# Token mixing two tiles behind the attention, with a batch's inner layer split behind the tile's normalisation

## The chip, the cores and the metric

The kernel runs on one core of one Trainium2 chip. The metric is the device time of one execution in microseconds (us); the time before is the median of three executions. Five engines matter: TensorE (PE, with its weight loads shown as PEld), VectorE (DVE), ScalarE (ACT), GpSimd (POOL), and SyncE (SP), which issues most of the DMAs. Each engine works through its own queue in the order in which the program was written; semaphores tie the queues together.

## The reference, cut to what matters

```python
# q, k, v: (8 batches, 8 heads, 576 positions, 64)
scores = q @ k.T / 8, masked to the 64 latest positions
attn   = softmax(scores) @ v                     # -> x: (8, 576, 512)
xt = x.transpose(0, 2, 1)
h  = np.maximum(xt @ w_tok1, 0.0) @ w_tok2       # token mixing, inner layer of 256
u  = x + h.transpose(0, 2, 1)
h2 = np.maximum(u @ w_ch1, 0.0) @ w_ch2          # channel mixing, inner layer of 1536
out = u + h2
```

So there is a windowed attention, then a token-mixing layer over the positions of each batch (two matrix products with a ReLU between), then a channel-mixing layer. The products of the two mixing layers are done with each operand split into a high part, rounded to a shorter mantissa, and the low remainder: three matmuls (high·high, low·high, high·low) stand for one.

## The kernel before, in words

**Tiles.** The 8 batches of 576 positions are cut into 36 attention tiles of 128 positions, nine to a pair of batches (`tile_blocks`, L65). Tiles 0 to 3 of a pair belong to its first batch, 5 to 8 to its second, and tile 4 holds 64 positions of each. So a batch's last attention tile is number 4 or 8 of its pair.

**Steps.** The loop of L462 makes step i (from -1 to 36). In step i stand the second half of the attention of tile i and the beginnings of later tiles:

- `pt_transpose(i, 0)`, `(i, 1)` (L297): four transposes each on PE into a PSUM tile `pp`, and a copy by ACT to `pt`. The index u in 0, 1 stands for the even and the odd heads.
- `softmax(i + 1, u)` and `softmax_exp(i + 1, u)` (L270, L288): DVE scales and masks the scores (`e`) and takes the row maximum (`nm`); ACT then runs four exponentials.
- `av(i, pts)` (L308): 32 small matmuls into `xp`. The first 16 read `pt(i, 0)`, the second 16 read `pt(i, 1)`. `norm(i)` (L325) then makes the tile's `x` on DVE.
- `qk(i + 2)` (L250): the scores `s` of the tile after next, 32 small matmuls.

Threaded through these are the token-mixing layer and the weight conversion:

- `split_x(n)` (L331): ACT casts `x` of tile n to `xhi`, POOL subtracts to give `xlo`. For a tile number 4 these are two casts and two subtractions on half the partitions each (L338, L339).
- `tok1(n)` (L423): tile n's part of the first token-mixing product, six matmuls of 512 columns into the two PSUM tiles `h` of its batch (four for a tile 4, whose second half belongs to the next batch and is added with tile 5, which then has ten). After a batch's last tile, `finish_h` (L364) makes the ReLU: two ACT instructions to `hhi`, two DVE instructions to `hlo`, and queues the batch's eight *pieces*.
- `tok2` (L380), one piece: two or three transposes of `x`, then six matmuls of 256 or 320 columns into one PSUM tile `up`, and a copy to `u` by ACT. There is a single `up` buffer until step 35, when `up_tags` gets four more (L471). `PIECES` (L44) says how many pieces a step runs in its first slot (behind the four exponentials of u = 0, L495) and its second (behind `qk`, L521); without an entry it is one and one.
- `JOBS` (L43) says in which steps weights are converted: one job in every step up to 5, then in the steps whose number three does not divide. In the step behind such a one ACT has a cast `w1hi` more.

**The plan.** `tok1_plan` (L456 to L460) gives tile n of the token mixing to step n + 1 from step 4 on, after a first stretch with one tile a step. `split_x(n)` stands at the end of step n, behind that step's `norm`, `qk` and second piece (L522 to L524), unless the plan lets it stand early, in the middle of a step (L489 to L492); it may only if tile n's `norm` was in an earlier step.

**After the loop** the last pieces are run, and then the channel mixing (L585 on): 9 chunks of 512 positions, each with 144 matmuls (`gp`, L593) and 144 more (`op`, L629), PE almost without a gap.

Of the kernel before, what the change touches and what calls it, by code (L numbers as in the profile page):

```python
# [40 lines left out]


JOBS = {i: 1 if i < 6 or i % 3 else 0 for i in range(-1, 37)}  # L43
PIECES = {32: (1, 0), 33: (1, 0), 34: (1, 0), 35: (3, 0), 36: (2, 1)}  # L44

TOK1_FROM, TOK1_SLOW, TOK2_FROM = 2, 4, 7

N_PE, N_EARLY = 7, 4

# [25 lines left out]
def mixer_kernel(ctx: ExitStack, tc: tile.TileContext, qh, kh, vh, wt1, wt2, wc1, wc2, out):  # L75
# [37 lines left out]
    with ExitStack() as actx:  # L113
# [8 lines left out]
        def load_k(i):  # L122
            p, t = divmod(i, TPP)
            if t in (0, 4):
                b = 2 * p + (t == 4)
                kbs[b] = pq.tile([P, H // 2, (NBLK + 1) * BLK], F32, name=f"k{b}", tag="k", bufs=2)
                if b != 0:
                    nc.sync.dma_start(kbs[b], kh[b])

        def load_q(i):  # L130
            qr = pq.tile([P, H // 2, 2, BLK], F32, name=f"q{i}", tag="q", bufs=5)
            nc.sync.dma_start(qr, qh[i])
            loaded[i] = [qr, None]

        def load_v(i):
            vt = pq.tile([P, 2, H, D], F32, name=f"v{i}", tag="v", bufs=3)
            nc.sync.dma_start(vt, vh[i])
            loaded[i][1] = vt
# [158 lines left out]
        def pt_transpose(i, u):  # L297
            pp = ps.tile([P, 4, P], F32, name=f"pp{i}_{u}", tag="pt")
            e = e_sb.pop((i, u))
            for h in range(4):  # L300
                nc.tensor.transpose(pp[:, h], e[:, h], ident)  # L301
            pt = pa.tile([P, 4, P], F32, name=f"pt{i}_{u}", tag="ptsb", bufs=4)
            nc.scalar.copy(pt, pp)  # L303
            return pt
# [13 lines left out]
        def recip(i):  # L318
            _, sm = st.pop(i)
            ri = pa.tile([P, H], F32, name=f"ri{i}", tag="ri", bufs=2)  # L320
            nc.vector.tensor_scalar_add(ri, sm, 1e-9)
            nc.vector.reciprocal(ri, ri)
            return ri

        def norm(i, xp, ri):  # L325
            x = pa.tile([P, H, D], F32, name=f"x{i}", tag="x", bufs=12)
            nc.vector.tensor_mul(x, xp, ri.unsqueeze(2).to_broadcast([P, H, D]))
            xs[i] = x.rearrange("p h d -> p (h d)")
# [17 lines left out]
        def tok1_part(i, b, rows, slot, first, last):  # L346
            xhi, xlo = xhl[i]
            if first:
                h_ps[b] = [ps.tile([P, C], F32, name=f"h{b}_{tt}", tag="h") for tt in range(NTT)]
            for tt in range(NTT):  # L350
                if rows is full:
                    combos = ((t1hi, xhi), (t1hi, xlo), (t1lo, xhi))
                else:
                    x = xhi if rows is top else xlo
                    combos = ((t1hi, x), (None, x))
                for n, (w, x) in enumerate(combos):
                    w, o = (t1z[:, rows is bottom], 0) if w is None else (w, slot * DT)
                    nc.tensor.matmul(h_ps[b][tt], w[:, o + tt * P:o + (tt + 1) * P], x,  # L358
                                     start=first and n == 0, stop=last and n == len(combos) - 1)
# [3 lines left out]
        def finish_h(b):  # L363
            hh = []  # L364
            for tt in range(NTT):
                hp = h_ps[b][tt]
                hi = pa.tile([P, C], F32R, name=f"hhi{b}_{tt}", tag=f"hhi{tt}", bufs=2)
                lo = pa.tile([P, C], F32R, name=f"hlo{b}_{tt}", tag=f"hlo{tt}", bufs=2)
                nc.scalar.activation(hi, hp, AF.Relu)
                nc.vector.scalar_tensor_tensor(out=lo, in0=hp, scalar=0.0, in1=hi.bitcast(F32),  # L370
                                               op0=ALU.max, op1=ALU.subtract)
                hh.append((hi, lo))
            h_ps.pop(b)
            for half in range(2):
                for ct in range(NCT):
                    pieces.append((b, half, ct, hh))
# [36 lines left out]
        def store_u():  # L413
            while stores:
                us, g0, n = stores.pop(0)
                a = 0
                while a < n:
                    j, o = divmod(g0 + a, CHUNK)
                    m = min(n - a, CHUNK - o)
                    (nc.sync if g0 < (B - 1) * S - 320 else nc.scalar).dma_start(u_dram[j][:, :, o:o + m], us[:, :, a:a + m])  # L420
                    a += m

        def tok1(i):  # L423
            p, t = divmod(i, TPP)
            b0, b1 = 2 * p, 2 * p + 1
            if t < 4:
                tok1_part(i, b0, full, t, t == 0, False)
            elif t == 4:
                tok1_part(i, b0, top, 4, False, True)
                finish_h(b0)  # L430
            else:
                if t == 5:
                    tok1_part(i - 1, b1, bottom, 4, True, False)
                tok1_part(i, b1, full, t - 5, False, t == 8)
                if t == 8:
                    finish_h(b1)

        def run_pieces(k):
            for _ in range(min(k, len(pieces))):
# [15 lines left out]
        load_v(1)  # L455
        tok1_plan, n = {}, 0  # L456
        for i in range(TOK1_FROM, NT + 1):
            m = min(n + (1 if i < TOK1_SLOW else 2), i)
            tok1_plan[i] = range(n, m)
            n = m  # L460
        qk(0)
        for i in range(-1, NT + 1):  # L462
            if 0 <= i and i + 2 < NT:
                load_v(i + 2)
            if 3 <= i + 3 < NT:
                load_q(i + 3)
            if i + 4 < NT:
                load_k(i + 4)
            store_u()
            n_jobs = JOBS[i]  # L470
            if i == NT - 1:  # L471
                up_tags += [("s", 2), ("pt", 2)]
            have = len(pieces)
            n_pieces = PIECES.get(i, (1, 1) if i >= TOK2_FROM else (0, 0))
            pts = []
            early = i < N_EARLY
            if 0 <= i < NT:
                pts.append(pt_transpose(i, 0))
                if early:
                    pts.append(pt_transpose(i, 1))  # L480
            if i + 1 < NT:
                softmax(i + 1, 0)
            if early and i > 0:
                norm(*normed.pop())
            if 0 <= i < NT:
                ri = recip(i)
            while to_finish:
                job_finish()
            for n in tok1_plan.get(i + 1, ()):  # L489
                last_use = n - NX + ((n - NX) % TPP == 4)  # L490
                if n < i and last_use not in tok1_plan.get(i, ()):
                    split_x(n)  # L492
            if i + 1 < NT:
                softmax_exp(i + 1, 0)
            run_pieces(min(have, n_pieces[0]))  # L495
            have = min(have, len(pieces))
            if not early:
                for _ in range(n_jobs):
                    job_convert_a()
            if 0 <= i < NT and not early:  # L500
                pts.append(pt_transpose(i, 1))
            if i + 1 < NT:
                softmax(i + 1, 1)
            if early:
                for _ in range(n_jobs):
                    job_convert_a()
            for n in tok1_plan.get(i, ()):
                tok1(n)
            if i + 1 < NT:
                softmax_exp(i + 1, 1)  # L510
            for _ in range(n_jobs):
                job_convert_b()
            if 0 <= i < NT:
                xp = av(i, pts)
                if i + 1 < N_EARLY:
                    normed = [(i, xp, ri)]
                else:
                    norm(i, xp, ri)
            if i + 2 < NT:
                qk(i + 2)  # L520
            run_pieces(min(have, n_pieces[1]))  # L521
            for n in tok1_plan.get(i + 1, ()):  # L522
                if n not in xhl:
                    split_x(n)  # L524
            while to_load and len(to_convert) < 2 and i < NT - 2:
                job_load()
            if i == NT - 1:
                while to_convert or to_convert_b or to_finish:
                    job_convert_a()
                    job_convert_b()  # L530
                    job_finish()
                qctx.close()
                pu = uctx.enter_context(tc.tile_pool(name="pu", bufs=1, side="right", reuse_waits="tile"))
                ul = {0: load_u(0, pu)}
# [136 lines left out]
```

## Time and profile before

| what | value |
|---|---|
| median of three runs | 878.97 us (878.91 to 879.26) |
| the profiled execution's own time | 880.53 us |
| its span, first to last instruction | 878.7 us |
| mean granted TensorE clock | 0.993 |
| busy over the span | PE 850.6, PEld 702.6, DVE 378.3, ACT 307.5, POOL 105.3 us |
| start of step 0's `av` / of step 35's `av` | 14.80 / 268.34 us |
| first `gp` matmul of the channel mixing | 283.36 us |

The profile is one execution. A row of the timeline gives start, duration, engine, line, operation, output<-inputs, the shape (partitions x elements), a count, and in brackets the engine's idle time ahead of it with what ended it. Consecutive instructions of one kind are merged into a row. PE's matmuls are pipelined: a matmul of 512 columns shows 0.39 us, but the next one starts 0.23 us behind it. So it is starts that tell PE's pace, and an idle time of PE is shown only as far as it goes beyond the end of the matmul before. A row of the waits gives who waited for whom, the total in us, the number of times and the longest. The steps below are named by their number i; the attention's steps take about 7 us each.

### The profile page before, as it was taken

Reading aid. Unit: us, or ns where it says so; the run is one execution under the profiler, and the core shown is the slowest. Engines: PE = TensorE matmul, PEld = TensorE weight load, DVE = VectorE, ACT = ScalarE, POOL = GpSimd, SP = SyncE. Lnnn points to the kernel's source line nnn. Section 1 sums busy time; section 2 is a strip of 40 time slices with the busy share of each in tenths; the row PEclk is TensorE's granted clock in tenths of the full one; section 3 lists DMA queues with packets and bytes.
Section 4 is the critical chain, followed back from the end, with each engine's and each line's share of the span. In section 5 each row is a group of like instructions: output and inputs, shape, how many; then the busy total and the mean of one; then the engine's idle time right before and its main releaser. Section 6 shows DMA issues by size and latency. Waiting matters only on the chain.

```text
span 878.7 us, 14566 instructions
## 1 busy us (share of the span) xinstructions
PE 850.6 (97%) x6002; PEld 702.6 (80%) x6002; DVE 378.3 (43%) x701; ACT 307.5 (35%) x966; POOL 105.3 (12%) x109
## 2 busy tenths in 40 slices
PE   6889999989989999999999999999999999999998
PEld 4668878868879878888888888888888888888887
DVE  5979878878874795220220220220220220220211
ACT  5778777878875341120120220220220220220200
POOL 3433343433332000000000000000000000000000
PEclk9989999999999999999999999999999999999999
DMA  9566667567535531100100100100100101100001
GB/s 322 195 203 229 200 235 244 183 235 246 182 127 167 182 106 57 60 7 30 60 13 24 60 13 25 60 13 25 60 12 31 54 13 39 46 13 37 0 13 37
DMA packets 39907, 84.69 MB, mean 96 GB/s; under 512 B 5281, under 2 KB 18337, under 8 KB 37921
## 3 DMA queue, kind: packets, MB, share of 16 engines
q1 hardware_dynamic: 37728, 81.93, 27.9%
q10 hardware_dynamic: 2112, 1.84, 0.6%
q8 instruction: 47, 0.77, 0.4%
q14 instruction: 20, 0.16, 0.1%
HBM read 64.09 MB, written 19.66 MB: 95 GB/s over the span
## 4 chain that ended last, share of the span: by engine, by line
PE 83%; DVE 8%; ACT 4%; POOL 2%; issue 2%; DMA 1%; POOLq 0%; SPq 0%; DVEq 0%; ACTq 0%
PE op L629 33%; PE gp L593 30%; PE h L358 5%; PE up L400 4%; PE s L266 4%; PE xp L313 3%; PE up L393 2%; POOL xlo L94 2%; PE pp L301 1%; ACT u L405 1%; DVE r L200 1%; DMA u_dram<-u 1%; DVE c L197 1%; ACT xhi L91 1%; ACT e L294 1%
## 5 line engine op out<-in xcount | busy, mean ns | idle before, releaser
L597 ACT ACTIVATE ghi<-gp 128x512 fp32r<-128x512 f32 x108 | 64.5, 597 | 432.2 <-PE gp L593 431.9
L629 PE MATMUL op<-ghi,w2lo 128*128 128x512 f32 (+1 forms) x444 | 170.9, 385 | 1.9 <-DVE w2lo L94 1.9
L629 PE MATMUL op<-glo,w2hi 128*128 128x512 f32 (+1 forms) x444 | 170.9, 385 | 0.0
L629 PE MATMUL op<-ghi,w2hi 128*128 128x512 f32 (+1 forms) x444 | 170.8, 385 | 0.0
L593 PE MATMUL gp<-ulo,w1hi 128*128 128x512 f32 x432 | 168.1, 389 | 0.0
L593 PE MATMUL gp<-uhi,w1hi 128*128 128x512 f32 x432 | 168.1, 389 | 0.0
L593 PE MATMUL gp<-uhi,w1lo 128*128 128x512 f32 x432 | 168.0, 389 | 0.0
L598 DVE SCALAR_TENSOR_TENSOR glo<-gp,ghi 128x512 fp32r<-128x512 f32 x108 | 74.5, 690 | 187.7 <-ACT ghi L597 187.7
L631 DVE TENSOR_TENSOR uf<-op,uf 128x512 f32<-128x512 f32 (+1 forms) x37 | 25.0, 677 | 243.7 <-PE op L629 243.7
L629 PEld LDWEIGHTS op<-ghi,w2lo 128*128 128x128 f32 x444 | 83.9, 189 | 18.8 <-DVE w2lo L94 2.3
L629 PEld LDWEIGHTS op<-ghi,w2hi 128*128 128x128 f32 x444 | 83.8, 189 | 16.6
L629 PEld LDWEIGHTS op<-glo,w2hi 128*128 128x128 f32 x444 | 83.8, 189 | 16.5
L593 PEld LDWEIGHTS gp<-uhi,w1hi 128*128 128x128 f32 x432 | 81.1, 188 | 16.9
L593 PEld LDWEIGHTS gp<-uhi,w1lo 128*128 128x128 f32 x432 | 81.1, 188 | 16.8
L593 PEld LDWEIGHTS gp<-ulo,w1hi 128*128 128x128 f32 x432 | 81.1, 188 | 16.8
L294 ACT ACTIVATE e<-e,nm 128x128 f32<-128x128 f32 x232 | 90.5, 396 | 8.0 <-DVE nm L286 8.0
L94 POOL TENSOR_TENSOR xlo<-x,xhi 128x512 fp32r<-128x512 f32 x32 | 42.9, 1340 | 66.3 <-ACT xhi L91 66.0
L313 PEld LDWEIGHTS xp<-v,pt 128*64 128x64 f32 x1152 | 37.4, 137 | 16.4 <-ACT pt L303 6.3
L266 PE MATMUL s<-k,q 64*64 64x128 f32 x1152 | 43.7, 287 | 2.4 <-DVE c L197 1.9
L313 PE MATMUL xp<-v,pt 128*64 128x64 f32 x1152 | 43.1, 226 | 2.7 <-ACT pt L303 2.4
L294 ACT ACTIVATION_READ_ACCUMULATOR e<-e,nm 128x1 f32 x232 | 44.8, 193 | 0.0
L303 ACT COPY pt<-pp 128x512 f32<-128x512 f32 x72 | 41.8, 587 | 6.4 <-PE pp L301 6.3
(79 smaller groups left out, 1002.7 us busy)
## 6 DMA issues: line engine op xcount, KB each, us to landing
v<-vh SPq DMA_DIRECT2D x36, 512.0 KB, 3.8
raw<-wc SPq DMA_DIRECT2D x32, 384.0 KB, 4.4
q<-qh SPq DMA_DIRECT2D x36, 256.0 KB, 4.6
k<-kh SPq DMA_DIRECT2D x7, 1280.0 KB, 8.0
out<-uf SPq DMA_DIRECT2D x35, 256.0 KB, 2.3
uf<-u_dram SPq DMA_DIRECT2D x8, 1024.0 KB, 5.6
u_dram<-u SPq DMA_DIRECT2D x7, 512.0 KB, 3.7
k<-kh SPq DMA_DIRECT2D x5, 256.0 KB, 6.2
```

The costliest lines, as they stand in the source:

```text
L94: eng_lo.tensor_sub(lo, src, hi.bitcast(F32))
L266: nc.tensor.matmul(s[u][half * BLK:(half + 1) * BLK, j], qt[r, j, half], kbs[b][r, j, n * BLK:n * BLK + P], start=not on_pe, stop=True, sk ...
L294: nc.scalar.activation(e[:, h], src[:, h], AF.Exp, bias=nm[:, g:g + 1], scale=by, accum_out=sm[:, g:g + 1])
L303: nc.scalar.copy(pt, pp)
L313: nc.tensor.matmul(xp[half * BLK:(half + 1) * BLK, h], pts[h % 2][:, h // 2, half * BLK:(half + 1) * BLK], vt[:, half, h], start=True, sto ...
L358: nc.tensor.matmul(h_ps[b][tt], w[:, o + tt * P:o + (tt + 1) * P], x, start=first and n == 0, stop=last and n == len(combos) - 1)
L400: nc.tensor.matmul(up[:, :n], hx[:, cs], w[:, tt * S + s0:tt * S + s0 + n], start=False, stop=(k == 6), skip_group_check=True)
L593: nc.tensor.matmul(gp, w[:, ct * F + ft * P:ct * F + (ft + 1) * P], x[:, ct], start=(k == 0), stop=(k == 3 * NCT - 1))
L597: nc.scalar.activation(ghi, gp, AF.Relu)
L598: nc.vector.scalar_tensor_tensor(out=glo, in0=gp, scalar=0.0, in1=ghi.bitcast(F32), op0=ALU.max, op1=ALU.subtract)
L629: nc.tensor.matmul(op, w[:, ct, ft], x[:, cols], start=(k == 0), stop=(k == 3 * NFT - 1))
L631: nc.vector.tensor_add(uf[:, ct, cols], op, uf[:, ct, cols])
```

## The change

It does four things.

1. `tok1_plan` gives tile n of the token mixing to step n + 2 in place of n + 1, up to step 33. In step 34 the lag is made up: this step has tiles 32 and 33. By this, `split_x(n)` moves from the end of step n to the middle of step n + 1 (L489 to L492 apply now).
2. `finish_h` is no longer called inside `tok1`; the batch is put on a list, and the two ACT and two DVE instructions are written behind the step's `norm`, ahead of `qk`.
3. `PIECES` has two pieces in the first slot of step 34 in place of one.
4. What follows from 1: a batch's eight pieces become available one step later. Steps 15 and 24 now have no piece to run in either slot (before: 23 and 32); step 32 and step 33 have one each (before: none and one), step 34 two (before: one).

```diff
-PIECES = {32: (1, 0), 33: (1, 0), 34: (1, 0), 35: (3, 0), 36: (2, 1)}
+PIECES = {32: (1, 0), 33: (1, 0), 34: (2, 0), 35: (3, 0), 36: (2, 1)}
...
-TOK1_FROM, TOK1_SLOW, TOK2_FROM = 2, 4, 7
+TOK1_FROM, TOK1_SLOW, TOK1_CATCH_UP, TOK2_FROM = 2, 4, 34, 7
...
+        to_finish_h = []
...
                 tok1_part(i, b0, top, 4, False, True)
-                finish_h(b0)
+                to_finish_h.append(b0)
...
                 if t == 8:
-                    finish_h(b1)
+                    to_finish_h.append(b1)
...
-            m = min(n + (1 if i < TOK1_SLOW else 2), i)
+            m = min(n + (1 if i < TOK1_SLOW else 2), i - (i < TOK1_CATCH_UP))
...
                     norm(i, xp, ri)
+            while to_finish_h:
+                finish_h(to_finish_h.pop(0))
             if i + 2 < NT:
                 qk(i + 2)
```

Three places in the order of the instructions show it. The first is ACT's queue from the second piece's copy of step 11 to the second `pt` of step 12, a step with a weight cast. Numbers behind a name are the tile's (and u), or the batch's and the half's and column block's for `u` and `up`; the last number is the buffer's. Before:

```order
L405 COPY u1_0_1435<-up1_0_1_1504 128x256
L91 CAST xhi11_1514<-x11_1484 128x512
L303 COPY pt12_0_1529<-pp12_0_1524 128x512
L91 CAST w1hi_66<-w10_1462 128x384
L294 ACTIVATE e13_0_1533,sum13_1532<-e13_0_1533,nm13_1531 128x128 x4
L405 COPY u1_0_1435<-up1_0_2_1545 128x256
L303 COPY pt12_1_1560<-pp12_1_1555 128x512
```

The same stretch of ACT's queue now:

```order
L406 COPY u1_0_1427<-up1_0_1_1498 128x256
L304 COPY pt12_0_1519<-pp12_0_1514 128x512
L92 CAST w1hi_66<-w10_1456 128x384
L92 CAST xhi11_1531<-x11_1478 128x512
L295 ACTIVATE e13_0_1523,sum13_1522<-e13_0_1523,nm13_1521 128x128 x4
L406 COPY u1_0_1427<-up1_0_2_1539 128x256
L304 COPY pt12_1_1554<-pp12_1_1549 128x512
```

The cast `xhi` of tile 11 went behind the first `pt` and the weight cast; between the first row and the last stand the same five instructions as before.

The second place is ACT's queue in step 34, from the odd heads' exponentials of tile 34 to the second `pt`. Before:

```order
L294 ACTIVATE e34_1_4006,sum34_3976<-e34_1_4006,nm34_3975 128x128 x4
L91 CAST xhi33_4062<-x33_4042 128x512
L303 COPY pt34_0_4071<-pp34_0_4066 128x512
L294 ACTIVATE e35_0_4075,sum35_4074<-e35_0_4075,nm35_4073 128x128 x4
L405 COPY u6_0_3997<-up6_0_1_4085 128x256
L303 COPY pt34_1_4104<-pp34_1_4099 128x512
```

The same stretch now:

```order
L295 ACTIVATE e34_1_3982,sum34_3948<-e34_1_3982,nm34_3947 128x128 x4
L370 ACTIVATE hhi6_0_4012<-h6_0_3534 128x512
L370 ACTIVATE hhi6_1_4016<-h6_1_3535 128x512
L92 CAST xhi33_4038<-x33_4010 128x512
L304 COPY pt34_0_4048<-pp34_0_4043 128x512
L295 ACTIVATE e35_0_4052,sum35_4051<-e35_0_4052,nm35_4050 128x128 x4
L406 COPY u6_0_4071<-up6_0_0_4062 128x256
L406 COPY u6_0_4071<-up6_0_1_4073 128x256
L304 COPY pt34_1_4092<-pp34_1_4087 128x512
```

Batch 6's two ReLU instructions now stand here (before, in step 32), and the copies of two pieces stand behind tile 35's exponentials in place of one.

The third place is PE's queue in step 34 around the pieces, up to the token mixing of batch 7. Before:

```order
L400 MATMUL up6_0_1_4085<-t2hi_134,hlo6_1_3910 128x256
L301 MATMUL pp34_1_4099<-ident_65,e34_1_4006 128x128 x4
L358 MATMUL h7_0_4009<-xhi33_4062,t1hi_132 128x512
L358 MATMUL h7_0_4009<-xlo33_4063,t1hi_132 128x512
L358 MATMUL h7_0_4009<-xhi33_4062,t1lo_133 128x512
L358 MATMUL h7_1_4010<-xhi33_4062,t1hi_132 128x512
L358 MATMUL h7_1_4010<-xlo33_4063,t1hi_132 128x512
L358 MATMUL h7_1_4010<-xhi33_4062,t1lo_133 128x512
L313 MATMUL xp34_4125<-v34_3862,pt34_0_4071 64x64 x8
```

The same place now, from the first piece's last matmul on:

```order
L401 MATMUL up6_0_0_4062<-t2hi_134,hlo6_1_4017 128x256
L394 MATMUL up6_0_1_4073<-ident_65,x27_3322 128x128
L394 MATMUL up6_0_1_4073<-ident_65,x28_3438 128x128
L401 MATMUL up6_0_1_4073<-t2hi_134,hhi6_0_4012 128x256
L401 MATMUL up6_0_1_4073<-t2lo_135,hhi6_0_4012 128x256
L401 MATMUL up6_0_1_4073<-t2hi_134,hlo6_0_4013 128x256
L401 MATMUL up6_0_1_4073<-t2hi_134,hhi6_1_4016 128x256
L401 MATMUL up6_0_1_4073<-t2lo_135,hhi6_1_4016 128x256
L401 MATMUL up6_0_1_4073<-t2hi_134,hlo6_1_4017 128x256
L302 MATMUL pp34_1_4087<-ident_65,e34_1_3982 128x128 x4
L359 MATMUL h7_0_4097<-xlo31_3849,t1hi_132 128x512
```

A second piece follows the first on PE directly, into the same single `up` buffer, and behind `pp34_1` stand sixteen `h` matmuls (tiles 32 and 33 with the half of 31) where six stood.

## The prediction

> **What bounds the kernel now.** I read the page first, for the share of each engine.
>
> ```profile
> PE 850.6 (97%) x6002; PEld 702.6 (80%) x6002; DVE 378.3 (43%) x701; ACT 307.5 (35%) x966; POOL 105.3 (12%) x109
> ```
>
> PE is the bound over the whole, but the change touches only the attention (to 283 us of 879), and there the question is what PE waits for. So I read the waits next.
>
> ```profile
> PEld h L358 <- POOL xlo L94: 9.6, 19, 1.2
> ...
> PEld h L358 <- POOL xhi L339: 5.8, 4, 2.0
> ...
> PE xp L313 <- ACT pt L303: 2.4, 5, 0.7
> ```
>
> PE's weight loads for the token mixing wait 9.6 + 5.8 = 15.4 us for `split_x`: this is the most that the change can remove. Five times `av` waits for `pt` from ACT. Whether the 15.4 us come back depends on how far behind that second wait is, so I read a steady step with a weight cast on the timeline, step 12: ACT's rows, then PE's.
>
> ```profile
> 97.18 0.37 ACT L405 COPY u<-up 128x256 f32<-128x256 f32 x1 [1.45 <-PE up L400]
> 97.45 0.62 ACT L91 CAST xhi<-x 128x512 fp32r<-128x512 f32 x1
> 97.97 0.59 ACT L303 COPY pt<-pp 128x512 f32<-128x512 f32 x1
> 98.44 0.52 ACT L91 CAST w1hi<-w 128x384 fp32r<-128x384 f32 x1
> 98.86 0.41 ACT L294 ACTIVATE e<-e,nm 128x128 f32<-128x128 f32 x1
> ...
> 100.41 0.36 ACT L405 COPY u<-up 128x256 f32<-128x256 f32 x1
> 100.66 0.59 ACT L303 COPY pt<-pp 128x512 f32<-128x512 f32 x1
> ```
>
> ```profile
> 98.96 0.47 PE L358 MATMUL h<-xhi,t1hi 128*128 128x512 f32 x1
> 99.50 0.50 PE L358 MATMUL h<-xlo,t1hi 128*128 128x512 f32 x1
> ...
> 100.85 1.15 PE L313 MATMUL xp<-v,pt 128*64 128x64 f32 x32
> ```
>
> PE loses about 0.3 us between the first `h` matmul and the one that reads `xlo`. Then `av` runs through without a break. But its second half, which reads the second `pt`, begins half a microsecond in, at about 101.35, and that `pt` ends at 101.25. ACT arrives 0.1 us ahead of PE. It got there without idling from 97.18 on, through 4.07 us of work that PE's piece of the step before released. A step without a weight cast has more room:
>
> ```profile
> 107.28 0.59 ACT L303 COPY pt<-pp 128x512 f32<-128x512 f32 x1
> ...
> 107.96 1.15 PE L313 MATMUL xp<-v,pt 128*64 128x64 f32 x32
> ```
>
> Here `pt` ends at 107.87 and the second half begins at about 108.45, 0.6 us later. So in the steady steps two waits stand almost in line, and the change removes only the first.
>
> **The steady steps (8 to 13, 17 to 22, 26 to 31).** The cast `xhi` moves on ACT from ahead of the first `pt` to behind it; the work between 97.18 and 101.25 stays the same. The first `pt` now follows the copy directly and has to wait for its transposes: four of them take 0.66 (the row at 258.19 below) from about the piece's end, the copy gives way after 0.27, so ACT idles at most 0.3 there; I take 0.15. In a step with a cast PE therefore gains the 0.1 that ACT is early and loses 0.15: 12 steps x 0.05 = +0.6. Five of the six without a cast have a wait for `xlo`, which goes: 5 x -0.3 = -1.5. In steps 10, 19 and 28 the ReLU now stands on ACT between the exponentials and the second piece's copy, and on DVE behind `norm` and ahead of the next tile's `e`; who waits for that copy is PE's next piece. ACT idles 1.45 us ahead of this copy (row 97.18), the two instructions take 1.07 (row 248.60 below), so it fits but for some 0.1 each: +0.3. On POOL `xlo` now stands behind the weight's subtraction, with most of a step until PE reads it, and on SP the stores of `u` are issued a step later, hundreds of us ahead of their loads: nothing for both. Sum -0.6, between -8 (nearly all waits of these steps return) and +2 (no gain, 12 bubbles).
>
> **Steps without pieces.** Before, these are 23 and 32, and the longest waits (2.0, 1.2) lie at them. Now they are 15 and 24, where PE has only transposes, `h`, `av` and `qk`, so ACT sets the pace, with the ReLU on top. I take -0.45 for each: -0.9, between -4 (two times 2.0) and +1. The start, steps 4 to 7, is bound by ACT and DVE in the same way, and there half the `h` work only moves later: +0.3, between -1.5 and +1.5.
>
> **The end, steps 32 to 35.** Up to step 31 PE has now done six `h` matmuls and two pieces fewer; they return here, and I follow the queues. Before, on PE:
>
> ```profile
> 256.07 1.15 PE L313 MATMUL xp<-v,pt 128*64 128x64 f32 x32
> 257.15 1.10 PE L266 MATMUL s<-k,q 64*64 64x128 f32 x32
> 258.19 0.66 PE L301 MATMUL pp<-ident,e 128*128 128x128 f32 x4
> 258.68 0.38 PE L393 MATMUL up<-ident,x 128*128 128x128 f32 x2
> ...
> 259.97 0.48 PE L358 MATMUL h<-xhi,t1hi 128*128 128x512 f32 x1
> ...
> 261.52 1.40 PE L313 MATMUL xp<-v,pt 128*64 128x64 f32 x32
> ```
>
> On ACT (ReLU of batch 6, first exponential of tile 35, the piece's copy) and on DVE (`hlo`, the row maximum of tile 35):
>
> ```profile
> 248.60 1.07 ACT L369 ACTIVATE hhi<-h 128x512 fp32r<-128x512 f32 x2
> ...
> 259.80 0.40 ACT L294 ACTIVATE e<-e,nm 128x128 f32<-128x128 f32 x1 [0.27 <-DVE nm L286]
> ...
> 261.36 0.35 ACT L405 COPY u<-up 128x256 f32<-128x256 f32 x1
> ```
>
> ```profile
> 249.23 1.29 DVE L370 SCALAR_TENSOR_TENSOR hlo<-h,hhi 128x512 fp32r<-128x512 f32 x2 [2.16 <-ACT hhi L369]
> ...
> 259.02 0.69 DVE L286 TENSOR_REDUCE nm<-e 128x4 f32<-128x512 f32 x1
> ```
>
> From the middle of step 33's `av` (256.6) to step 34's `av` it was 4.9 us. Now count from that middle. The scores start at 0.55, the transposes at 1.6, the first piece at 2.1. ACT has the four exponentials of tile 34 until 1.4 (1.55 for four, 98.86 to 100.41), then the ReLU until 1.9 and 2.5; DVE makes `hlo` until 2.65 and 3.3, and only then `e` and the maximum of tile 35 (0.69 each), until 4.7. The first piece needs the second `hlo` and ends at 3.6. The second piece needs the same `up` buffer, so it waits for the first one's copy; this copy stands on ACT behind tile 35's exponentials, which wait for the maximum and run from 4.8 to 6.35; with 0.3 for the copy the second piece starts at 6.7. PE stands still for **3.1 us**, and all that is queued behind waits with it. Then a piece with its transposes (1.3, from 258.68 to 259.97) and sixteen `h` matmuls at 0.25 (six take 1.55, from 259.97 to 261.52), 3.9: step 34's `av` starts at 11.9. That is +7.0. Against it steps 32 and 33 lose their two long waits for the split (2.0 and 1.2) and get some 1.4 of waits for `pt` and a piece back: -1.8; step 35, whose `av` came behind a `pt`, wins 0.4. Sum +4.8, between +3 (ACT through early) and +5.5.
>
> The Trainium skill, Perfetto Trace Analysis, section Optimizing Tensor Performance (Matmuls), says that independent matmul groups should rotate through different PSUM banks so that emptying one overlaps the next. By this rule, the two pieces in one buffer lose their overlap; with a second buffer the stall would go and the sum would end near 879.5.
>
> **The clock.** A stretch of the channel mixing shows what a stall does:
>
> ```profile
> 320.95:324.37 3.42, 1.56 (x7) 0.98 (x7) 3.32 (x7) 1.53 (x4) 0.00 (x0) 1.00 0.35 85
> 324.37:327.78 3.41, 3.41 (x10) 2.66 (x9) 3.27 (x9) 0.08 (x1) 0.00 (x0) 0.50 0.23 89
> ```
>
> The columns are length, busy time of PE, PEld, DVE, ACT, POOL, and the granted clock. PE was busy for 1.56 of 3.42 us, and in the next 3.41 it ran at half the clock, on a full load: 1.7 us lost. A stall of 3.1 us leaves one such stretch just as idle, maybe a second partly, with sixteen `h` matmuls right behind. I take 2.2, between 0 and 2.9. The Trainium skill, TensorE: Matmul & The Clock Gate, Part 1, has the clock fall after an idle window of about 3.4 us; the row above has it fall on a window that was nearly half busy, and by the page's rule the sum would be 2.2 lower.
>
> **Sum.** -0.6 - 0.9 + 0.3 + 4.8 + 2.2 = +5.8 us. The profiled execution (880.53, of which span 878.7 and 1.8 around it) would take 886.3; it stands 1.6 above the median of the runs, to which I add the same: 878.97 + 5.8 = **884.8 us**. A measurement of this kernel can tell about 0.2% from no change, 1.8 us.
>
> **The rivals.**
> 1. *ACT has more room than I read, and the waits return in full* (faster). All 15.4 but the 3.2 counted at the end return: 878.97 - 12.2 + 7.0 = 873.8. It decides from 8.8 us on, when 7.0 and 1.8 are covered. For it speaks the size of the waits; against it the 0.1 us of step 12. Chance 0.13.
> 2. *Half of it returns*: 878.97 - 6.1 + 7.0 = 879.9, or a dearer middle with a shorter stall, as `hlo` might not hold tile 35's maximum up: also about 879 to 880, no change that can be told. Chance 0.15.
> 3. *The clock stays full behind the stall* (it needs a whole idle stretch): 884.8 - 2.2 = 882.6. Against it the rows above. Chance 0.17.
> 4. *The clock falls also at the start or in steps 15 and 24*, where PE is left with little work: 1.7 us once or twice, 887.5. Chance 0.10.
>
> The forecast itself keeps 0.45. Slower has 0.45 + 0.17 + 0.10 = 0.72, same 0.15, faster 0.13. The range reaches from 878.0, which leaves out rival 1 and a little of rival 2, to 889.0, rival 4 with the dear ends of the end and the clock.
>
> **What would show it.** Right: `h` no longer waits for POOL, and `xp` waits for `pt` in two of three steady steps; in step 34 a gap of about 3 us on PE ahead of the second piece, released by ACT's copy, and half the clock behind it; step 31's `av` about one microsecond earlier than before, step 35's four to six later. Wrong: step 31's `av` several microseconds earlier (rival 1), or no such gap in step 34.

## The result and the profile after

The changed kernel takes **887.32 us** (median of four runs, 886.99 to 887.69); the kernel before, measured beside it, 879.12 us (four runs). The ratio is 1.009, with a 95% interval from 1.0074 to 1.0106: slower, where 884.8 us was forecast. Of all executions, two ran in a slower state (one of before at 1399.44 us, one of the run with step 4 filled at 955.10 us) and are left out of every time below. The profiled execution took 887.69 us with a span of 885.9, which is 7.2 more than the span before. PE's busy time over the span hardly changed (851.3 us after, 850.6 before), and work at half the clock counts as busy; the rest of the 7.2 us is more time in which PE stands.

The waits first. These are rows of the waits view for PE's weight loads and for its matmuls (total, times, longest):

```profile
PEld xp L314 <- ACT pt L304: 18.5, 26, 2.6
...
PEld h L359 <- POOL xlo L95: 0.4, 1, 0.4
```

```profile
PE xp L314 <- ACT pt L304: 14.3, 20, 2.5
...
PE up L394 <- ACT u L406: 2.9, 1, 2.9
```

The wait of `h` for the split has gone from 9.6 to 0.4 us. In its place `av` waits for ACT's `pt`: 20 times and 14.3 us among the matmuls, where it was 5 times and 2.4. Between 66 and 250 us it is 13 times and 7.9 us, where it was twice and 1.1. Among the matmuls, the wait of a piece for the copy of the `up` buffer is new.

To see in which stage time is lost, I take the start of the second `pt` copy of a step as a mark. Before, in steps 8, 31 and 35:

```profile
71.69 0.59 ACT L303 COPY pt<-pp 128x512 f32<-128x512 f32 x1
...
240.03 0.59 ACT L303 COPY pt<-pp 128x512 f32<-128x512 f32 x1
...
267.11 0.59 ACT L303 COPY pt<-pp 128x512 f32<-128x512 f32 x1
```

The same marks after:

```profile
74.12 0.58 ACT L304 COPY pt<-pp 128x512 f32<-128x512 f32 x1
...
242.37 0.58 ACT L304 COPY pt<-pp 128x512 f32<-128x512 f32 x1
...
275.49 0.59 ACT L304 COPY pt<-pp 128x512 f32<-128x512 f32 x1
```

With the marks of steps 13, 17, 22 and 26 as well (107.28, 138.08, 173.84 and 204.26 before; 110.25, 140.18, 176.32 and 206.23 after) the span divides up like this:

| stage, from mark to mark | before | after | difference | by PE | forecast |
|---|---|---|---|---|---|
| start to step 8 | 71.69 | 74.12 | +2.4 | +2.4 | +0.3 |
| steady: 8 to 13, 17 to 22, 26 to 31 | 107.12 | 108.41 | +1.3 | +0.1 | -0.6 |
| 13 to 17 and 22 to 26 (after: one step without pieces in each; before: in the second alone) | 61.22 | 59.84 | -1.4 | -0.7 | -0.9 |
| 31 to 35 | 27.08 | 33.12 | +6.0 | +6.5 | +7.0 (4.8 and the clock's 2.2) |
| 35 to the end of the span | 611.59 | 610.41 | -1.2 | -1.2 | 0 |
| sum | 878.7 | 885.9 | +7.2 | +7.2 | +5.8 |

The mark is ACT's, and in a step without a weight cast ACT is ahead of PE (before by 0.6 us, in the prediction's row at 107.28). So the difference books some of PE's time one stage too early or too late. The column "by PE" takes the start of the scores behind a step's `av` in place of the mark (steps 8, 13, 17, 22, 26 and 31: 72.95, 109.04, 139.44, 175.68, 205.60 and 241.86 before; 75.36, 111.59, 141.43, 177.66, 207.48 and 243.71 after) and in step 35, which has no scores, the start of `av` (268.34 and 276.72).

**A steady step.** Step 12, ACT's copies and PE's `av`:

```profile
99.69 0.35 ACT L406 COPY u<-up 128x256 f32<-128x256 f32 x1
100.08 0.59 ACT L304 COPY pt<-pp 128x512 f32<-128x512 f32 x1
100.69 0.51 ACT L92 CAST w1hi<-w 128x384 fp32r<-128x384 f32 x1
...
103.18 0.35 ACT L406 COPY u<-up 128x256 f32<-128x256 f32 x1
103.43 0.58 ACT L304 COPY pt<-pp 128x512 f32<-128x512 f32 x1
```

```profile
103.00 0.69 PE L314 MATMUL xp<-v,pt 128*64 128x64 f32 x16
104.06 0.69 PE L314 MATMUL xp<-v,pt 128*64 128x64 f32 x16 [0.37 <-ACT pt L304]
```

Now nothing holds `h` up, so PE reaches `av` earlier and stops in its middle: the second half waits 0.37 us for the second `pt`. From the piece's copy to the end of that `pt` ACT needs 4.32 us (99.69 to 104.01), where it was 4.07. The whole stretch from step 8's scores to step 31's says the same: PE was busy there for 159.16 us, 3.5 less than before (162.71), above all since two pieces come later now, and yet it took 168.35 us, where it was 168.91.

**Step 34.** PE, DVE and ACT:

```profile
260.21 0.38 PE L401 MATMUL up<-t2hi,hlo 128*128 128x256 f32 x1
263.53 0.69 PE L394 MATMUL up<-ident,x 128*128 128x128 f32 x2 [2.94 <-ACT u L406]
...
266.01 0.76 PE L359 MATMUL h<-xlo,t1hi 128*128 128x512 f32 x1
...
270.15 1.15 PE L314 MATMUL xp<-v,pt 128*64 128x64 f32 x32
```

```profile
258.87 1.29 DVE L371 SCALAR_TENSOR_TENSOR hlo<-h,hhi 128x512 fp32r<-128x512 f32 x2 [0.59 <-ACT hhi L370]
260.08 0.68 DVE L284 SCALAR_TENSOR_TENSOR e<-s,mask 128x512 f32<-128x512 f32 x1
260.79 0.69 DVE L287 TENSOR_REDUCE nm<-e 128x4 f32<-128x512 f32 x1
```

```profile
261.58 0.40 ACT L295 ACTIVATE e<-e,nm 128x128 f32<-128x128 f32 x1 [1.26 <-DVE ri L322]
...
263.13 0.35 ACT L406 COPY u<-up 128x256 f32<-128x256 f32 x1
```

The chain reads as forecast: `hlo` until 260.16, then `e` and the maximum until 261.48, four exponentials until 263.23, the copy, and at 263.53 the second piece. The stall is 2.94 us. The clock answers, in the windows view (length, busy time of PE, PEld, DVE, ACT, POOL, granted clock, DMA share, GB/s). The granted clock changes only at times that lie a multiple of 3.41 us apart; a *stretch* is the time between two such neighbours.

```profile
259.78:263.20 3.42, 0.82 (x4) 0.44 (x4) 3.28 (x9) 2.16 (x11) 1.27 (x1) 1.00 0.00 0
263.20:266.61 3.41, 3.08 (x14) 2.98 (x15) 2.28 (x5) 0.82 (x4) 0.87 (x1) 0.50 0.01 2
```

PE was busy for 0.82 us of the first stretch; in the next it worked 3.08 us at half the clock, which is 1.5 us lost.

**The start.** PE in step 4, and the stretches around it:

```profile
38.82 0.69 PE L314 MATMUL xp<-v,pt 128*64 128x64 f32 x16
41.97 1.12 PE L314 MATMUL xp<-v,pt 128*64 128x64 f32 x16 [2.46 <-ACT pt L304]
```

```profile
37.92:41.33 3.41, 1.59 (x21) 0.99 (x19) 3.31 (x8) 2.32 (x11) 2.23 (x2) 1.00 0.40 118
41.33:44.74 3.41, 2.77 (x30) 2.00 (x34) 3.27 (x8) 2.10 (x11) 0.47 (x2) 0.50 0.23 18
44.74:48.16 3.42, 3.42 (x37) 3.09 (x30) 1.36 (x5) 0.86 (x2) 0.70 (x1) 0.50 0.94 383
```

Before, step 4 had twelve `h` matmuls; now it has six, and PE stands for 2.46 us in the middle of `av`. The second `pt` comes hardly later (41.33, before 41.16), but from 41.33 to 48.16 the clock was at half: the 32 matmuls of the scores at 44.18 took 1.99 us, where those at 43.48 before took 1.10. Before, PE had more work at this place and full clock behind it; there the clock fell later, and stayed at half from 51.30 to 58.13:

```profile
37.65:41.06 3.41, 2.27 (x9) 1.34 (x8) 2.84 (x9) 2.70 (x10) 2.29 (x2) 1.00 0.47 144
...
47.88:51.30 3.42, 1.75 (x37) 1.29 (x36) 3.32 (x8) 2.94 (x12) 0.19 (x1) 1.00 0.94 334
51.30:54.71 3.41, 2.71 (x32) 2.38 (x33) 3.27 (x7) 1.27 (x5) 1.39 (x2) 0.50 0.69 223
```

So both kernels lose clock at the start: before 6.8 us at half, after 10.2 (41.33 to 48.16 and 54.98 to 58.40).

### The profile page after: what moved, and what is told of

Same layout as the page of the kernel before. It is cut to its first block, busy times and chain, and to the rows that moved or that the text cites. A ratio compares the mean times of both kernels' runs of the same rounds, so it can differ in the third digit from the quotient of the medians.

```text
span 885.9 us, 14563 instructions
## 1 busy us (share of the span) xinstructions
PE 851.3 (96%) x6002; PEld 705.9 (80%) x6002; DVE 376.8 (43%) x701; ACT 308.7 (35%) x966; POOL 105.2 (12%) x109
## 4 chain that ended last, share of the span: by engine, by line
PE 73%; DVE 12%; ACT 11%; issue 2%; DMA 2%; POOLq 0%; SPq 0%; POOL 0%; ACTq 0%; DVEq 0%
PE op L634 33%; PE gp L598 29%; ACT e L295 6%; PE s L267 3%; PE up L401 2%; PE xp L314 2%; ACT pt L304 2%; PE h L359 1%; DVE e L284 1%; DVE nm L287 1%; DVE c L188 1%; PE pp L302 1%; DVE c L189 1%; PE up L394 1%; ACT xhi L92 1%
## 5 line engine op out<-in xcount | busy, mean ns | idle before, releaser
L314 PE MATMUL xp<-v,pt 128*64 128x64 f32 x1152 | 47.2, 228 | 15.0 <-ACT pt L304 14.3
L302 PE MATMUL pp<-ident,e 128*128 128x128 f32 x288 | 44.9, 286 | 0.0
```

Of the source, the lines that this page charges most:

```text
L314: nc.tensor.matmul(xp[half * BLK:(half + 1) * BLK, h], pts[h % 2][:, h // 2, half * BLK:(half + 1) * BLK], vt[:, half, h], start=True, sto ...
```

## The experiments

My theory: `av`'s wait for ACT stands right behind the split's wait, so the removed wait does not come back; the loss is the single `up` buffer in step 34, the half clock behind it, and half clock at the start. The rivals: ACT (or DVE) sets the pace whatever the buffer and the clock; or the moved ReLU is what costs. The median of before, measured beside them, was 878.74 us for the first four runs, 879.58 for the next four and 879.18 for the last three. Ratios are against that.

**A second buffer in step 34.**

```diff
-            if i == NT - 1:
-                up_tags += [("s", 2), ("pt", 2)]
+            if i == NT - 2:
+                up_tags += [("s", 2)]
+            if i == NT - 1:
+                up_tags += [("pt", 2)]
```

> The changed kernel, but the second piece of step 34 goes to a buffer of the scores (free there) and not to the single up buffer. Theory (the loss at the end is the single buffer, and the half clock behind the stall): the stall of 2.9 us ahead of the second piece falls to 0.5 or less, no half clock follows at 263 us, and the time falls by about 4, from 887.3 to 883.3 us. Rival (ACT sets the pace of step 34 in any case): the wait moves to the second pt ahead of av, and the time stays at 886 or more.

Measured: 883.59 us, ratio 1.0059 (1.0042 to 1.0077). PE in step 34:

```profile
259.25 0.44 PE L394 MATMUL up<-ident,x 128*128 128x128 f32 x2 [0.22 <-DVE e L284]
...
264.43 1.15 PE L314 MATMUL xp<-v,pt 128*64 128x64 f32 x32
```

The stall fell to 0.22 us, no half clock followed, and `av` came 5.2 us after the second piece began (259.25 to 264.43) in place of 6.6. The theory's number holds. The run also shows something on the start: up to step 33 this program is the changed kernel's, its wait in step 4 is the same 2.46 us, and yet its clock did not fall there:

```profile
37.97:41.38 3.41, 1.70 (x21) 1.10 (x19) 3.31 (x9) 2.21 (x9) 2.12 (x2) 1.00 0.55 157
41.38:44.80 3.42, 2.67 (x53) 2.07 (x54) 3.28 (x8) 2.20 (x11) 0.48 (x2) 1.00 0.10 41
```

PE was busy for 1.70 of 3.41 us in place of 1.59, since the work began 0.1 us later against the stretches. Step 8's mark stood at 72.60, 1.5 earlier than in the changed kernel's profile. So of the 3.7 us between the two medians a part may be the start's clock; in the profiles, the marks 31 to 35 took 28.97 us against 33.12, which is 4.2 for the buffer, the half clock behind the stall included. Before it was 27.08, so 1.9 us of the end's loss are still there.

**The ReLU's place alone**, on the kernel before.

```diff
-                finish_h(b0)
+                to_finish_h.append(b0)
...
-                    finish_h(b1)
+                    to_finish_h.append(b1)
...
+            while to_finish_h:
+                finish_h(to_finish_h.pop(0))
             if i + 2 < NT:
                 qk(i + 2)
```

> The kernel before, with the ReLU of a batch written behind the step's norm and nothing else changed. Theory (the ReLU's place costs little; now it stands behind four exponentials on ACT, and the next step's first piece waits for hlo a little, eight times 0.3 us at most): 879.1 to 881.5 us, likeliest 880. Rival (the moved ReLU is what costs): 884 us or more.

Measured: 878.36 us, ratio 0.9996 (0.9986 to 1.0005): no difference. On the kernel before, the moved ReLU costs nothing that can be told; not even the small loss that I expected.

**The lag alone**: the changed kernel with the ReLU back in the token mixing.

```diff
-                to_finish_h.append(b0)
+                finish_h(b0)
...
-                    to_finish_h.append(b1)
+                    finish_h(b1)
```

> The changed kernel with the ReLU back inside the token mixing; only the lag, the catching up and the second piece in step 34 are left. Theory (the lag and the end cost): batch 6's ReLU no longer stands ahead of tile 35's maximum in step 34, so the stall there is shorter, 1.5 in place of 2.9 us, and all else stays: about 885.9 us (884.5 to 887). Rival (the moved ReLU is what costs): 881 us or less.

Measured: 886.44 us, ratio 1.0088 (1.0069 to 1.0107). The lag and the end cost, not the ReLU. The stall of step 34 was 2.50 us where I expected 1.5. Counted from the second half of step 33's `av`, the second piece began 5.7 us later (256.42 to 262.16), 0.9 earlier than in the changed kernel (256.86 to 263.53); but the first piece, which no longer waits for `hlo`, was over 0.5 earlier too, so PE stood for only 0.4 less. And what is left is not DVE's: ahead of tile 35's exponentials ACT idles 0.22 us here (1.26 in the changed kernel), and the rest of the chain is ACT's own queue.

**PE kept busy in step 4.**

```diff
             for h in [*range(0, H, 2), *range(1, H, 2)]:
+                if i == 4 and h == 1:
+                    for _ in range(8):
+                        nc.tensor.matmul(xp[:, 1::2], t1hi[:, :P], t1hi[:, :2 * P], start=True, stop=True)
```

> The changed kernel with eight more matmuls of 256 columns in step 4, between the two halves of av where PE waits 2.46 us for pt; they write into the part of xp that the second half overwrites, so the work that is computed stays as it is. Theory (the loss of 2.2 us at the start is the half clock from 41.3 to 48.2 us, which follows a window in which PE was busy under half of the time): the window is now busy for over 0.8, the clock stays full, and of the 2.2 us some 1.6 come back: 885.7 us. Rival (the start is paced by ACT and DVE, whatever the clock): 887.3 us, no change.

Measured: 884.28 us (884.18 to 886.16), ratio 1.0072 (1.005 to 1.0093). PE in step 4, and the stretches around it:

```profile
40.73 1.21 PE L315 MATMUL xp<-t1hi 128*128 128x256 f32 x8
43.26 0.69 PE L317 MATMUL xp<-v,pt 128*64 128x64 f32 x16 [1.31 <-ACT pt L304]
```

```profile
39.67:43.08 3.41, 2.27 (x27) 1.62 (x25) 3.27 (x9) 2.79 (x11) 1.97 (x2) 1.00 0.41 115
43.08:46.50 3.42, 3.24 (x59) 2.64 (x59) 3.32 (x8) 1.81 (x10) 0.77 (x1) 1.00 0.40 104
```

The stretch is now busy for two thirds (without the filling's 1.21 us it would be 0.31), and full clock follows. From step 4's mark to step 8's it is 31.12 us (42.61 to 73.73), where the changed kernel took 32.79 (41.33 to 74.12): 1.7 us came back, as expected, through matmuls that nobody needs. That is the part of the start's loss that the clock made. The kernel before took 30.53 between these marks, so 0.6 us are left, and as much in the run with the second buffer (31.12), whose clock was at half for 6.8 us there, as before. With the lag alone it was 30.33, so these 0.6 us seem to hang on the ReLU's place; that is one trace each. The other half of the 3.0 us between the medians is not the filling's: the stall of step 34, 2.9 us as ever, lay across two stretches in this profile, PE was busy for over half of each (2.03 and 1.87 us), and the clock stayed up there too.

**ACT relieved**: the changed kernel with the cast `xhi` on POOL.

```diff
-                split(nc.scalar, nc.gpsimd, xhi, xlo, xs[i])
+                split(nc.gpsimd, nc.gpsimd, xhi, xlo, xs[i])
```

> The changed kernel with the cast xhi of whole tiles on POOL and not on ACT, which takes 0.6 us from ACT's work between a piece's copy and the second pt in most steps. Theory (in the steady steps av is paced by ACT's second pt, 18.5 us of waits in 26 places): the waits for pt in steps 6 to 32 fall to under half, and some 5 us come back: 882 us (879 to 884.5). Rival (VectorE, busy for 6.0 of 7.2 us in such steps, or PE itself sets the pace): the wait only changes its name, 886.5 us or more.

Measured: 881.69 us, ratio 1.0029 (1.0013 to 1.0044), 5.6 less than the changed kernel.

```profile
PE xp L314 <- ACT pt L304: 9.4, 10, 2.4
```

The waits for `pt` fell from 20 places to 10 over the whole attention, and from 13 to 5 (7.9 to 4.4 us) between 66 and 250 us, a little less than I expected. The middle of the kernel gained although start and end kept their losses: from step 8's scores to step 31's it took 162.07 us, 6.3 less than the changed kernel. So it is ACT that paces `av` in the steady steps, and not DVE, whose work there is the same in both.

**The lag from step 8 on, with the second buffer.** The buffer's edit is the one above; the other is this:

```diff
-            m = min(n + (1 if i < TOK1_SLOW else 2), i - (i < TOK1_CATCH_UP))
+            m = min(n + (1 if i < TOK1_SLOW else 2), i - (8 <= i < TOK1_CATCH_UP))
```

> The changed kernel with the lag beginning in step 8 (steps 2 to 7 as before the change) and the second piece of step 34 in a buffer of the scores. Theory (start, middle and end add up: start 0, middle 0, end 2.0 as in the run with the second buffer): 881 us. Rival (the middle is not free: the lag costs something that the early steps hid): 883.5 us or more.

Measured: 882.29 us, ratio 1.0035 (1.0023 to 1.0047), 1.3 dearer than the sum. The profile names one cause:

```profile
121.73:125.14 3.41, 1.71 (x37) 1.14 (x35) 0.35 (x1) 3.41 (x15) 2.23 (x2) 1.00 0.64 197
125.14:128.55 3.41, 3.41 (x42) 3.08 (x40) 2.68 (x5) 2.13 (x9) 0.00 (x0) 0.50 0.68 192
```

Around step 15, which has no piece, PE was busy for half of a stretch, and the clock fell there; from step 8's scores to step 31's it took 169.34 us, 1.0 more than the changed kernel. This is the other place that rival 4 named.

**The split's wait removed in another way**: on the kernel before, the matmuls that read `xlo` behind those that read `xhi`.

```diff
+            if rows is full:
+                parts = [(0, t1hi, xhi), (0, t1lo, xhi), (1, t1hi, xhi), (1, t1lo, xhi), (0, t1hi, xlo), (1, t1hi, xlo)]
+                for n, (tt, w, x) in enumerate(parts):
...
+                return
```

> The kernel before, with a tile's two matmuls that read xlo behind the four that read xhi; the same six matmuls, nothing else moved. This takes the wait for xlo (9.6 us) away without any lag. Theory (two waits stand almost in line, ACT's second pt is 0.05 to 0.3 us behind in steps with a weight cast and 0.6 in the others): 12 times 0.1 and 6 times 0.3 come back, 876 us (874.5 to 878), and av's waits for pt grow. Rival (ACT has room, the waits return in full): 870 us or less.

Measured: 875.97 us, ratio 0.9963 (0.9949 to 0.9978). PE in step 12, the start of the second piece, and from the last `h` to the scores:

```profile
97.19 0.44 PE L400 MATMUL up<-ident,x 128*128 128x128 f32 x2
...
99.55 0.63 PE L354 MATMUL h<-xlo,t1hi 128*128 128x512 f32 x2
100.11 1.47 PE L313 MATMUL xp<-v,pt 128*64 128x64 f32 x32
101.50 1.10 PE L266 MATMUL s<-k,q 64*64 64x128 f32 x32
```

ACT's second `pt` in the same step:

```profile
100.24 0.59 ACT L303 COPY pt<-pp 128x512 f32<-128x512 f32 x1
```

In the kernel before, the same piece and the scores:

```profile
97.60 0.44 PE L393 MATMUL up<-ident,x 128*128 128x128 f32 x2
...
101.93 1.10 PE L266 MATMUL s<-k,q 64*64 64x128 f32 x32
```

This step shows it most plainly. Before, `av` began 3.25 us after the second piece (97.60 to 100.85) and took 1.15; now it begins 2.92 us after it (97.19 to 100.11) and takes 1.47. From the piece to the scores it is 4.33 us before and 4.31 now. The 0.3 us that `h` no longer waits are spent inside `av`: its second half would begin half a microsecond in, at about 100.6, and the second `pt` ends at 100.83. In all, 3.6 of 9.6 us came back, though only 1.2 us of waits for `xlo` are left. One part of the expectation failed: the listed wait of `xp` for `pt` did not grow (2.6 us in 5 places, 2.4 before), since a wait in the middle of `av` as short as this one shows as a longer `av` row and not as an idle time.

**ReLU and order together.** Both edits above on the kernel before.

> The kernel before with both the ReLU behind the norm and the xlo matmuls last. Theory (two small gains that add up, since the ReLU's place touches other steps): 875.5 us. Rival (they are paced by the same ACT chain, and only the larger one counts): the time of the run with xlo last alone.

Measured: 875.43 us, ratio 0.9952 (0.9932 to 0.9971). The interval overlaps that of the order alone, so whether the ReLU adds 0.5 us stays open.

**The three repairs together**, on the changed kernel.

```diff
-                split(nc.scalar, nc.gpsimd, xhi, xlo, xs[i])
+                split(nc.gpsimd if 7 <= i < 33 else nc.scalar, nc.gpsimd, xhi, xlo, xs[i])
...
-            m = min(n + (1 if i < TOK1_SLOW else 2), i - (i < TOK1_CATCH_UP))
+            m = min(n + (1 if i < TOK1_SLOW else 2), i - (8 <= i < TOK1_CATCH_UP))
...
+            if i == NT - 2:
+                up_tags += [("s", 2)]
             if i == NT - 1:
-                up_tags += [("s", 2), ("pt", 2)]
+                up_tags += [("pt", 2)]
```

> The changed kernel with all three repairs: the lag from step 8 on, the second piece of step 34 in a buffer of the scores, and the cast xhi of tiles 7 to 32 (other than a tile 4) on POOL. Theory (ACT's second pt paces av once the split no longer does, so the lag pays only with ACT relieved): start 0, middle -6.5 and end +2 as in the runs with one repair each, about 875 us, 4 faster than the kernel before. Rival (the lag gains nothing beyond its own repairs): 879 us, the time of the kernel before.

Measured: 875.21 us, ratio 0.9953 (0.9936 to 0.9971). With all three repairs the lagged kernel is faster than the kernel before. Whether the lag itself gains, or the cast on POOL would gain as much without it, is not shown: the kernel before with the cast on POOL was not run.

**PE kept busy in step 5**, on the run with ReLU and order, and on the run with the three repairs.

```diff
+            if i == 5:
+                junk = ps.tile([P, 512], F32, name="junk", tag="up", bufs=1)
+                for _ in range(8):
+                    nc.tensor.matmul(junk, t1hi[:, :P], t1hi[:, :512], start=True, stop=True)
             if i + 2 < NT:
                 qk(i + 2)
```

> The kernel before with the ReLU behind the norm and the xlo matmuls last, and with eight more matmuls of 512 columns in step 5 ahead of the scores, where PE waits about 2 us for ACT's exponentials; they write into the up buffer, which nothing uses there, so the work that is computed stays as it is. Theory (the half clock from 53.9 us on follows the half-idle window that this wait makes): no half clock before 60 us, and 1.7 us or more come back: 873.5 us. Rival (the early steps are paced by ACT and DVE): 875.4 us, no change.

Measured: 874.13 us, ratio 0.9941 (0.9925 to 0.9957). Without the filling it was 875.43 and 0.9952, and the intervals overlap, so the medians do not tell the two apart. The traces do. PE in step 5, and two windows around it (3.5 and 3.4 us, not on the clock's edges):

```profile
51.23 2.14 PE L533 MATMUL junk<-t1hi 128*128 128x512 f32 x8
```

```profile
50.50:54.00 3.50, 3.39 (x44) 2.59 (x48) 3.33 (x8) 2.04 (x11) 0.48 (x1) 1.00 0.76 255
54.00:57.40 3.40, 3.40 (x41) 2.89 (x31) 3.28 (x8) 2.66 (x8) 1.82 (x2) 1.00 0.33 128
```

No half clock is left there, where the run without the filling had it from 53.86 to 57.27, and the marks 4 to 8 are 28.24 us apart in place of 29.32.

> The run with the three repairs and, in step 5, the eight more matmuls. Theory (the gains add up): 873 us. Rival (clock and lag share the same slack at the start): 875 us or more.

Measured: **872.23 us**, ratio 0.9921 (0.9906 to 0.9937), the fastest version, 7.0 us under the kernel before and 15 under the changed one. It is 3.0 less than the three repairs without the filling, and here the runs' ranges do not overlap; but in the two profiles the marks 4 to 8 give 1.0 of it (28.97 and 27.93), and more lies behind the attention, where the other's clock fell at 320.03 and this one's did not. Its five runs lie within 1.1 us (871.81 to 872.88); those of the kernel with the cast on POOL, whose profile has half-clock stretches in three places of the attention, within 4.5 (879.73 to 884.23).

## Why the prediction was right, and where its sizes were off

**The steady steps: right in the mechanism, 0.7 us too good.** The step said that two waits stand almost in line and that the change removes only the first. The waits of after, the run with `xlo` last and the run with the cast on POOL show it from three sides. Of the 18 steady steps, 9 have a listed wait of `xp` for `pt`, where two of three were forecast. The term was -0.6 and measured +0.1 by PE, in the 15 of these steps that lie between the marks. Over all 18, from the scores of one step to those of the next, the six steps without a weight cast gained 1.5 us, where 1.2 was forecast with the ReLU, and the twelve with one lost 2.0, where it was 0.6. So what was mis-sized is the 0.05 of a step with a cast; it was 0.16. ACT's work from copy to `pt` grew by 0.25 in step 12, of which I had taken 0.15 for the wait for the transposes; the first row behind that `pt`, the weight cast, comes another 0.1 late.

**Steps without pieces: right** (-0.7 by PE for -0.9), though the expectation that they stay at full clock was luck: in one of the runs above it fell there.

**The end: right in every link, 0.5 too dear.** The stall was 2.94 us for 3.1, released by ACT's copy; the half clock cost 1.5 for 2.2, because one stretch fell and not a part of a second. From the middle of step 33's `av` to step 34's it was 13.3 us (256.86 to 270.15), for the 11.9 of the count and the clock's 1.5. Steps 32 and 33 gave back 1.5 (from the scores of step 31 to those of step 33: 15.29 us before, 13.77 after) for 1.8. Step 35's `av` came 8.4 us later (276.72, before 268.34), where four to six was the sign: to the end's 6.5 come the 1.9 by which step 31 was late already. (Sixteen `h` matmuls at 0.25 are 4.0 and not the 3.9 of the sum; at full clock, in the run with the second buffer, they took 3.84, from 260.59 to 264.43.) The Trainium skill, Perfetto Trace Analysis, section Optimizing Tensor Performance (Matmuls), has independent groups rotate through different PSUM banks; the run with a second buffer agrees: the stall fell to 0.22 us, and the marks 31 to 35 came 4.2 us closer together.

**The start: the step that failed.** "+0.3, between -1.5 and +1.5" measured +2.4. The waits that I judged harmless (PE stands a little longer within a step that ACT and DVE bound) cost little in themselves, 0.6 us at most from mark 4 to mark 8, as the run with the second buffer shows: its step 8 came 1.5 earlier with the very same wait. What I did not price is that such a wait makes a stretch in which PE is busy under half of the time, and so half the clock: 10.2 us of it where there were 6.8, which cost 1.7. This is rival 4, to which I had given 0.10. That its time, 887.5 us, is the one that came is partly luck, since the other terms were off as well, in both directions. For the start above all, step 31's `av` did not come about one microsecond earlier, as I had written, but later: at 242.63 in place of 240.78.

**Behind the attention: not foreseen.** 1.2 us came back, for the half clock of before at 324.37 did not recur. The three traces with a half-clock stretch in the channel mixing took 611.6 to 612.5 us from step 35's mark to the end, the other ten 608.7 to 610.4. The wait for `w2lo` is still there (2.1 us), but it fell across two stretches, the emptier of them busy for 2.16 of 3.41:

```profile
331.46:334.87 3.41, 2.16 (x9) 1.79 (x10) 3.33 (x8) 0.97 (x2) 0.00 (x0) 1.00 0.39 115
```

So the sum of +5.8 against +7.2 in the profiles is made of errors that partly cancel: start +2.1, steady steps +0.7 and steps without pieces +0.2 against end -0.5 and channel mixing -1.2. The rest of the distance from 884.8 to 887.32 is that the profiled execution of before lies 1.6 above the median from which the forecast starts (880.53 against 878.97), the one of after only 0.4 above its own (887.69 against 887.32). Rival 1, that the waits return in full, is refuted by the run with `xlo` last: 3.6 of 9.6 us. What stays open is how often the clock falls in step 4 over many executions; each kernel has one trace. The granted clock of a whole execution is known for all: 0.991 to 0.994 in the changed kernel's four, 0.993 to 1.000 in the 45 of before that were measured beside the experiments, with a median of 0.996. So that the change loses clock is not the chance of one trace; in which step, only the traces say.

## What to carry to other kernels

A wait in the profile says what released an instruction, not what the release is worth: before removing it, read on the timeline when the next operand is ready. Here that was 0.1 us later, and taking 0.6 us of work off the engine that makes this operand brought the changed kernel 5.6 us, where the removed waits alone had brought none. When work is moved later, look where it lands, which buffer it shares there, and what is left at the place that it came from: at the start the clock cost more (1.7 us) than all else that the change did there (0.6).

## What the runs showed of the hardware

In each of these traces the granted clock changes only on a grid of 3.41 us, and it need not be an idle stretch that lowers it. From 30 us on, in the traces of the thirteen kernels, every stretch at full clock in which PE was busy for less than 0.46 of the time was followed by half the clock (0.82 of 3.42 us above, 1.56 of 3.42 in the prediction); between 0.46 and 0.51 it went both ways, six of 19 falling (1.59, 1.71, 1.75: half; 1.70: full); above that none fell (2.16, 2.27: full). A stretch at half the clock needs more to be the last: with PE busy for 0.71 to 0.83 of it another one followed (2.77, 2.71 of 3.41 above), with 0.90 and more full clock came back (3.08 of 3.41 above). The Trainium skill, TensorE: Matmul & The Clock Gate, Part 1, names an idle window of about 3.4 us and a window that runs freely against the kernel's start: the length and the free running agree with the rows, the idleness is too strict. The grid lies differently against the work in each trace: in the changed kernel and in the run with the second buffer a shift of 0.1 us went with 1.5 us at step 8, and eight needless matmuls in a wait took 1.0 to 1.7 us off the time between the marks 4 and 8 of three kernels.
